# The last stores spread over the DMA engines, and the last tokens' rows as f32r passes in the slots' matmul stream

## The chip, the cores and the metric

The program runs on one NeuronCore of a Trainium2 chip. The core has TensorE (PE, with its weight loads shown apart as PEld), VectorE (DVE), ScalarE (ACT), GpSimd (POOL) and the sync engine (SP, whose queue issues all the transfers here), and 16 DMA engines that move the data. The metric is the device time of one execution in microseconds (us), the median of several runs.

## The reference

Three layers follow one another. In the first, 8 batches of 8 heads have 512 sequence tokens and 32 state slots of 64 values each; tokens read from the slots and slots from the tokens by softmax attention. The heads are joined to 512 channels, and each batch is then a sequence of 544 rows: 512 tokens, and behind them 32 slots. The second layer multiplies a linear projection by the sigmoid of a causal convolution over five rows and projects the product. The third does the work around which the change lies:

```python
h = np.maximum(x @ w_in, 0.0)                    # 512 -> 1024 channels
hp = pad(h, one zero row on either side)
conv_out = sum(conv_w[k] * hp[:, k:k + S, :] for k in range(3))
gate = 1.0 / (1.0 + np.exp(-conv_out))
return (h * gate @ w_out).astype(np.float32)     # 1024 -> 512, out is (8, 544, 512)
```

The convolution of the third layer looks one row ahead. So the last token of a batch (row 511) depends on its first slot (row 512), and cannot be finished with the other tokens.

## The kernel before

The channels lie on the partitions and the rows of the sequence on the free axis. Batch after batch, the tokens go through the attention and the second layer; `z_unit(b, f)` then computes one of eight groups f of 128 of the 1024 channels for the 512 tokens of batch b (a matmul block with tile names z<-g,wp, lines 161 to 163), its convolution and gate, and `o_unit(b, f)` adds that group to the four output banks of the batch (tiles o<-w,f, lines 452 to 454). Most large products are made of three f32r passes: both operands are split into a high and a low part, and high x high, high x low and low x high are added. In `outer` the two passes of a group's high part are lines 452 and 453, and the one with its low part is 454. ScalarE makes the high part and GpSimd subtracts it from the value for the low part (`low`, line 135).

After the eighth group of a batch, `store` scales the four banks into SBUF and the sync engine writes them out: three stores of 128 rows, and one of 127, because the last token is missing.

The slots of all batches are collected and worked on together at the end, as one block of 8 x 32 = 256 rows: `s_val`, `s_z` (tiles zs and t2s) and `s_o` (tiles os<-w,fs). `s_z(f)` has 33 rows per batch: the last token and the 32 slots. The last token's gated value is copied by GpSimd into a small tile el, 128 channels x 8 groups x 32 columns, of which 8 are used and the rest is zero (line 584). `s_last` multiplies it by `w_out` with plain f32 matmuls (L602), four groups of channels side by side at four column places of the array, into a third bank. `s_sum` copies that bank to SBUF, and `s_pick` adds the four places with one more f32 matmul against a matrix of zeros and ones called pick (L610), and stores the 8 rows.

The order of the work at the end is written out by hand in the string `CLOSING`: letters stand for units (v, z and o for the slots' `s_val`, `s_z`, `s_o`; Z and O for the tokens of the last batch; E, A, S, T for the last tokens' `s_ends`, `s_last`, `s_sum`, `s_pick`), and a bar ends half a step. A scheduler then fixes the order on each engine. The engines work through their queues in that order; a new z or zs block needs the only PSUM bank of its kind, which ScalarE must have read before (L443, L572).

Of the kernel before, what the change touches and what calls it, by code (L numbers as in the profile page):

```python
# [9 lines left out]
F32 = mybir.dt.float32  # L10
F32R = mybir.dt.float32r
# [3 lines left out]
AF = mybir.ActivationFunctionType  # L15
ALU = mybir.AluOpType
AX = mybir.AxisListType
PSUM = bass.MemoryType.PSUM

P = 128  # L20
# [18 lines left out]

CLOSING = """  # L40
v2 | E | v0 O v1 v3 Z Z O Z | O Z z2 z0 | O | | o0 | z1 O | | o1 Z z3 o2 z4 O Z | O Z | | O Z o4
z5 z6 z7 O | | o5 A0 o3 | | A1 S O o67 | T
"""


# [14 lines left out]
def tile_cross_attention_gated_conv_ffn(  # L60
# [19 lines left out]
    nc = tc.nc  # L80
    B, H, S, D = x.shape
    NS = state.shape[2]
    DM = H * D
# [5 lines left out]
    NFT = DF // P  # L89
# [7 lines left out]
    const = ctx.enter_context(tc.tile_pool(name="const", bufs=1))  # L97
    xp = ctx.enter_context(tc.tile_pool(name="xp", bufs=4))
    att = ctx.enter_context(tc.tile_pool(name="att", bufs=2))
# [4 lines left out]
    ps_z = ctx.enter_context(tc.tile_pool(name="ps_z", bufs=1, space=PSUM))  # L104
# [3 lines left out]
    ident = const.tile([P, P], F32, name="ident")  # L108
# [5 lines left out]
    for q in range(4):  # L114
        for g in range(NG):
            w = (q ^ g) % 2
# [4 lines left out]
    wv = const.tile([P, NCT, DM], F32, name="wv")  # L121
    wp = const.tile([P, 2, NCT, DF], F32R, name="wp")
    hl = const.tile([P, NFT, B, 2], F32, name="hl")
    pick = const.tile([P, B], F32, name="pick")
    nc.vector.reduce_sum(pick, ident.rearrange("p (j m) -> p m j", m=32)[:, 0:B, :], axis=AX.X)
    sT = const.tile([P, NCT, B, NS + HALO], F32, name="sT")

    s_tile = lambda name, shape=(P, S): att.tile(list(shape), F32, tag="s", name=name, bufs=7)
    t_tile = lambda name, shape=(P, S): cv.tile(list(shape), F32, tag="t", name=name, bufs=6)
# [4 lines left out]
    def low(out, v, hi, e=None):  # L134
        (e or nc.gpsimd).tensor_tensor(out=out, in0=v, in1=hi.bitcast(F32), op=ALU.subtract)  # L135
# [50 lines left out]
    A = {}  # L186
# [225 lines left out]
    O = {}  # L412
    W2 = {}

    def inner(ps, gs, f):
        c = slice(f * P, (f + 1) * P)
        for k in range(NCT):
            three(ps, wp[:, 0, k, c], wp[:, 1, k, c], gs[k][:, 0], gs[k][:, 1], k == 0, k == NCT - 1)

    def conv2(t, h, f, dve=False):  # L420

        if dve:
            nc.vector.tensor_scalar_mul(t, h(1), cw2(f, 1))
        else:
            nc.scalar.activation(t, h(1), AF.Copy, scale=cw2(f, 1))  # L425
        for k in (0, 2):
            nc.vector.scalar_tensor_tensor(  # L427
                out=t, in0=h(k), scalar=cw2(f, k), in1=t, op0=ALU.mult, op1=ALU.add
            )

    def gate2(ft, t, h):
        nc.scalar.activation(t, t, AF.Tanh, scale=0.5)  # L432
        nc.vector.scalar_tensor_tensor(out=t, in0=t, scalar=1.0, in1=h, op0=ALU.add, op1=ALU.mult)  # L433
        if ft is not None:
            nc.scalar.activation(ft[:, 0], t, AF.Copy)  # L435
            low(ft[:, 1], t, ft[:, 0])
# [14 lines left out]
    def outer(ps, ft, c, f):  # L451
        nc.tensor.matmul(ps, ft[:, 0, c], W2[f][:, 0], start=(f == 0), stop=False)  # L452
        nc.tensor.matmul(ps, ft[:, 0, c], W2[f][:, 1], start=False, stop=False)  # L453
        nc.tensor.matmul(ps, ft[:, 1, c], W2[f][:, 0], start=False, stop=(f == NFT - 1))  # L454

    def store(ps, n, dst, spare=False):

        if spare:
            ob = t_tile("ob")
            nc.vector.tensor_scalar_mul(ob[:n], ps[:n], 0.5)  # L460
        else:
            ob = cv.tile([P, DM], F32, tag="ob", name="ob", bufs=3)
            nc.scalar.activation(ob[:n], ps[:n], AF.Copy, scale=0.5)
        nc.sync.dma_start(out=dst, in_=ob[:n])

    def o_unit(b, f):
        if f == 0:
            O[b] = [ps_o.tile([P, DM], F32, tag="o", name="o") for _ in range(NT)]
        ft = F.pop((b, f))
        for t in range(NT):  # L470
            outer(O[b][t], ft, slice(t * P, (t + 1) * P), f)
        if f == NFT - 1:
            for t in range(NT):
                n = P if t < NT - 1 else P - 1
                store(O[b][t], n, out[b, t * P : t * P + n, :], b == B - 1 and t % 2)
            O.pop(b)
# [62 lines left out]
    FS = {}  # L539
    OS = []  # L540
    PARTS = [(0, 3), (3, 3), (6, 2)]

    EL = []

    def s_ends():

        EL.append(s_tile("el", (P, NFT, 32)))
        nc.gpsimd.memset(EL[0], 0.0)

    def s_val(ct):  # L550
        t = t_tile("t1s", (P, B, NS))
# [15 lines left out]
    def s_z(f):  # L567
        ps = ps_z.tile([P, B, NS], F32, tag="z", name="zs")
        inner(ps.rearrange("p b n -> p (b n)"), GS, f)
        h = s_tile("hs", (P, B, NS + 3))  # L570
        nc.gpsimd.memset(h[:, :, NS + 2 : NS + 3], 0.0)
        nc.scalar.activation(h[:, :, 2 : NS + 2], ps, AF.Relu, scale=0.5)  # L572
        if f == NFT - 1:
            yield 1
        nc.gpsimd.tensor_copy(h[:, :, 0:2], hl[:, f])
        t = s_tile("t2s", (P, B, N1))
        conv2(t, lambda k: h[:, :, k : k + N1], f)
        yield LATE
        gate2(None, t, h[:, :, 1 : 1 + N1])
        FS[f] = xp.tile([P, 2, N], F32R, tag="xn", name="fs")  # L580
        hi, lo = (FS[f][:, i].rearrange("p (b n) -> p b n", b=B) for i in range(2))
        nc.scalar.activation(hi, t[:, :, 1:], AF.Copy)
        low(lo, t[:, :, 1:], hi)
        nc.gpsimd.tensor_copy(EL[0][:, f, 0:B], t[:, :, 0])

    def s_o(*fs):
        if 0 in fs:
            OS.extend(ps_a.tile([P, DM], F32, tag="a", name="os") for _ in range(3))
        for i in range(2):
            for f in fs:  # L590
                outer(OS[i], FS[f], slice(i * P, (i + 1) * P), f)
            if NFT - 1 in fs:
                store(OS[i], P, out[B // 2 * i : B // 2 * (i + 1), S:, :], i)

    def s_last(h):

        fs = range(4 * h, 4 * h + 4)
        for j in range(2):
            for f in fs:
                q = 32 * (f - 4 * h)  # L600
                w = W2[f][:, j].bitcast(F32)
                nc.tensor.matmul(OS[2][q : q + 32], EL[0][:, f], w, start=h == j == 0, stop=h == j == 1)  # L602

    def s_sum():
        OS.append(t_tile("ol"))
        nc.scalar.activation(OS[3], OS[2], AF.Copy)

    def s_pick():
        ps = ps_z.tile([P, DM], F32, tag="z", name="ol")
        nc.tensor.matmul(ps[0:B], pick, OS[3], start=True, stop=True)  # L610
        store(ps, B, out[:, S - 1, :])


    live = []
# [27 lines left out]
    def half_steps(text):  # L642
        return [h.split() for h in text.split("|")]
# [25 lines left out]

    def closing():  # L670

        fns = {"v": s_val, "z": s_z, "o": s_o, "E": s_ends, "A": s_last, "S": s_sum, "T": s_pick}
        f = {"Z": 0, "O": -2}
        for h in half_steps(CLOSING):
            lots = [], []
            for t in h:
                late_lot = t in ("Z", "O") or bool(lots[1])
                if t in ("Z", "O"):
                    fn = z_unit if t == "Z" else o_unit
                    u = (fn, B - 1, f[t]) if f[t] >= 0 else (fn, B - 2, NFT + f[t])  # L680
                    f[t] += 1
                else:
                    u = (fns[t[0]], *map(int, t[1:]))
                lots[late_lot].append(u)
            yield lots

    def product1(c):
# [7 lines left out]
        out=craw[0 : K1 * NCT].bitcast(U64), in_=conv1_w.rearrange("k (c p) -> (k c) p", p=P)  # L695
    )
    nc.sync.dma_start(
        out=craw[32 : 32 + K2 * NFT].bitcast(U64), in_=conv2_w.rearrange("k (c p) -> (k c) p", p=P)
# [47 lines left out]
    for b in range(B):  # L746
        if b == B - 1:
            for units, end in closing():
                step(*units, end=end)
            break  # L750
        units = ahead(b)
        if b == 0:
            units = [u + v for u, v in zip(units, among())]
        for f in range(NFT):
            o = [(o_unit, b, f - 2)] if f >= 2 else [(o_unit, b - 1, NFT - 2 + f)] if b else []
            step(*units[2 * f], end=o)
            step(*units[2 * f + 1], end=[(z_unit, b, f)])
        A.pop(b)
# [30 lines left out]
```

## Time and profile before

| | |
|---|---|
| median of 3 runs | 611.78 us (611.67 to 613.34) |
| the profiled execution, its own time | 611.8 us |
| its span, first to last instruction | 610.0 us |
| TensorE busy | 558.1 us, 91% of the span, 3044 matmul records |
| VectorE, ScalarE, GpSimd busy | 447.8, 351.1, 297.7 us |
| DMA | 37.84 MB, mean 62 GB/s |

An instruction is busy from its start to its end in the profile. Matmuls overlap: one of 512 columns is shown with about 0.39 us, but the next one starts 0.23 us after it. For TensorE the distance of starts is therefore what a matmul takes of the time, and the shown duration is not. An f32 matmul is shown as two records. The time of the profiled execution is 1.8 us longer than its span; what lies outside the span has no instruction of the program.

### The profile page before, as it was taken

How to read it: one execution, taken by the hardware profiler on the slowest of the kernel's cores; microseconds unless marked ns; L12 is line 12 of the kernel's file. 1: busy time of each engine (PE TensorE's matmuls, PEld its weight loads, DVE VectorE, ACT ScalarE, POOL GpSimd, SP SyncE). 2: the span in 40 equal slices, each digit the busy share in tenths (PEclk: the TensorE clock that was granted, in tenths of full speed). 3: DMA queues.
4: the chain of work that ended last, by engine and by line, in shares of the span. 5: the costliest groups of instructions: out<-in, count | busy, mean ns of one | idle time of the engine just before them, and what ended most of it. 6: DMA issues, size and time to landing. Idle time of an engine off the chain costs nothing.

```text
span 610.0 us, 8741 instructions
## 1 busy us (share of the span) xinstructions
PE 558.1 (91%) x3044; PEld 408.4 (67%) x3044; DVE 447.8 (73%) x715; ACT 351.1 (58%) x665; POOL 297.7 (49%) x378
## 2 busy tenths in 40 slices
PE   1866798889999999999999999999999999999990
PEld 0632566566567777786778677767876788886760
DVE  5798699698688588757995798499849886453440
ACT  6687466656565566556655756475547655553540
POOL 4675679277462544254625454554436435342220
PEclk9986899989999999999999999999999999999996
DMA  6976002720116003601350144013001000100011
GB/s 227 349 232 108 5 5 79 151 48 10 53 41 114 9 2 93 117 3 59 61 94 9 58 75 78 10 59 80 2 1 65 6 2 0 70 0 1 1 57 48
DMA packets 97670, 37.84 MB, mean 62 GB/s; under 512 B 90158, under 2 KB 90202, under 8 KB 97626
## 3 DMA queue, kind: packets, MB, share of 16 engines
q1 hardware_dynamic: 97626, 37.29, 24.0%
q8 instruction: 24, 0.39, 0.3%
q14 instruction: 20, 0.16, 0.1%
HBM read 28.36 MB, written 8.91 MB: 61 GB/s over the span
## 4 chain that ended last, share of the span: by engine, by line
PE 76%; DVE 13%; ACT 3%; issue 2%; DMA 2%; POOL 0%; SPq 0%; DVEq 0%; POOLq 0%; ACTq 0%
PE o L452 10%; PE z L161 9%; PE o L454 9%; PE o L453 9%; PE z L162 9%; PE z L163 9%; DVE t L386 2%; PE val L161 2%; PE val L162 2%; PE val L163 2%; PE xr L371 2%; DVE t L427 2%; PE sw L237 2%; PE sc L237 1%; PE os L602 1%
## 5 line engine op out<-in xcount | busy, mean ns | idle before, releaser
L427 DVE SCALAR_TENSOR_TENSOR t<-h,cw,t 128x512 f32<-128x512 f32 x128 | 117.1, 918 | 54.8 <-ACT t L425 53.6
L452 PE MATMUL o<-w,f 128*128 128x512 f32 x256 | 104.0, 408 | 1.8 <-ACT f L435 1.6
L135 POOL TENSOR_TENSOR f<-t,f 128x512 fp32r<-128x512 f32 x64 | 89.8, 1404 | 31.4 <-ACT f L435 30.8
L161 PE MATMUL z<-g,wp 128*128 128x512 f32 x256 | 103.7, 405 | 0.0
L162 PE MATMUL z<-g,wp 128*128 128x512 f32 x256 | 101.6, 397 | 0.2 <-POOL g L135 0.2
L163 PE MATMUL z<-g,wp 128*128 128x512 f32 x256 | 101.6, 397 | 0.0
L453 PE MATMUL o<-w,f 128*128 128x512 f32 x256 | 99.9, 392 | 0.0
L386 DVE SCALAR_TENSOR_TENSOR t<-xr,cw,t 128x510 f32<-128x510 f32 (+3 forms) x128 | 90.2, 741 | 4.9 <-ACT sT L379 4.2
L432 ACT ACTIVATE t<-t 128x512 f32<-128x512 f32 x64 | 40.6, 634 | 78.7 <-DVE t L427 78.5
L454 PE MATMUL o<-w,f 128*128 128x512 f32 x256 | 77.8, 397 | 0.1
L135 POOL TENSOR_TENSOR g<-v,g 128x512 fp32r<-128x512 f32 (+1 forms) x36 | 46.5, 1292 | 41.0 <-ACT g L397 40.9
L433 DVE SCALAR_TENSOR_TENSOR t<-t,h 128x512 f32<-128x512 f32 x64 | 53.4, 835 | 15.8 <-ACT t L432 15.2
L452 PEld LDWEIGHTS o<-w,f 128*128 128x128 f32 x256 | 48.0, 188 | 25.2 <-ACT f L435 7.6
L435 ACT ACTIVATE f<-t 128x512 fp32r<-128x512 f32 x64 | 40.5, 633 | 41.0 <-DVE t L433 40.8
L161 PEld LDWEIGHTS z<-g,wp 128*128 128x128 f32 x256 | 48.3, 189 | 16.5 <-issue 2.1
L162 PEld LDWEIGHTS z<-g,wp 128*128 128x128 f32 x256 | 48.3, 189 | 12.6 <-POOL n L218 0.8
L163 PEld LDWEIGHTS z<-g,wp 128*128 128x128 f32 x256 | 48.3, 189 | 11.9 <-issue 0.4
L454 PEld LDWEIGHTS o<-w,f 128*128 128x128 f32 x256 | 46.8, 188 | 11.7 <-issue 1.6
L453 PEld LDWEIGHTS o<-w,f 128*128 128x128 f32 x256 | 48.2, 188 | 9.1
L442 POOL MEMSET h<- 128x2 f32 x64 | 6.4, 101 | 92.4 <-DVE t L433 91.4
L443 ACT ACTIVATE h<-z 128x512 f32<-128x512 f32 x64 | 38.2, 597 | 22.7 <-PE z L163 20.9
L425 ACT ACTIVATE t<-h,cw 128x512 f32<-128x512 f32 x63 | 45.9, 729 | 1.4
(165 smaller groups left out, 1017.4 us busy)
## 6 DMA issues: line engine op xcount, KB each, us to landing
xn<-in_x_dram SPq DMA_DIRECT2D x32, 256.0 KB, 4.4
out_dram<-ob SPq DMA_DIRECT2D x26, 256.0 KB, 2.2
y<-in_x_dram SPq DMA_DIRECT2D x96, 64.0 KB, 2.3
wir<-in_moe_w_in_dram SPq DMA_DIRECT2D x8, 512.0 KB
wor<-in_moe_w_out_dram SPq DMA_DIRECT2D x8, 512.0 KB, 10.2
wmr<-in_moe_w_out_dram SPq DMA_DIRECT2D x4, 512.0 KB, 3.2
wvr<-in_moe_w_val_dram SPq DMA_DIRECT2D x4, 512.0 KB, 6.9
out_dram<-ob SPq DMA_DIRECT2D x8, 254.0 KB
```

Source lines behind the costliest of these rows:

```text
L135: (e or nc.gpsimd).tensor_tensor(out=out, in0=v, in1=hi.bitcast(F32), op=ALU.subtract)
L161: nc.tensor.matmul(ps, wh, mh, start=first, stop=False)
L162: nc.tensor.matmul(ps, wh, ml, start=False, stop=False)
L163: nc.tensor.matmul(ps, wl, mh, start=False, stop=last)
L386: nc.vector.scalar_tensor_tensor(out=t[:, n:], in0=ps[r][:, 0 : S - n], scalar=cw1(ct, k), in1=t[:, n:], op0=ALU.mult, op1=ALU.add,)
L425: nc.scalar.activation(t, h(1), AF.Copy, scale=cw2(f, 1))
L427: nc.vector.scalar_tensor_tensor(out=t, in0=h(k), scalar=cw2(f, k), in1=t, op0=ALU.mult, op1=ALU.add)
L432: nc.scalar.activation(t, t, AF.Tanh, scale=0.5)
L433: nc.vector.scalar_tensor_tensor(out=t, in0=t, scalar=1.0, in1=h, op0=ALU.add, op1=ALU.mult)
L452: nc.tensor.matmul(ps, ft[:, 0, c], W2[f][:, 0], start=(f == 0), stop=False)
L453: nc.tensor.matmul(ps, ft[:, 0, c], W2[f][:, 1], start=False, stop=False)
L454: nc.tensor.matmul(ps, ft[:, 1, c], W2[f][:, 0], start=False, stop=(f == NFT - 1))
```

## The change

There are two edits. In `store`, a store of more than 16 rows whose destination has the rows as its outer dimension is issued in two parts: the largest multiple of 16 rows, and the rest (127 becomes 112 and 15). The two stores of the slots are written with the slot number outside and the batch inside, 32 x 4 rows instead of 4 x 32; for that the slots are put in that order when their high and low parts are made (tile fs), so these are now written with a stride of four.

The second edit removes `s_last`, `s_sum`, `s_pick` and the pick matrix. The last tokens' values are split into a high part (ScalarE) and a low part (GpSimd), 128 x 8 each, and `s_o` sends them through `outer` as its third bank, 8 rows, with the same three f32r passes as the slots: 24 small f32r matmuls (os<-w,el) in place of the 16 f32 ones and the pick.

```diff
-z5 z6 z7 O | | o5 A0 o3 | | A1 S O o67 | T
+z5 z6 z7 O | | o5 o3 | | O o67
...
-    pick = const.tile([P, B], F32, name="pick")
-    nc.vector.reduce_sum(pick, ident.rearrange("p (j m) -> p m j", m=32)[:, 0:B, :], axis=AX.X)
...
-        nc.sync.dma_start(out=dst, in_=ob[:n])
+        even = n // 16 * 16
+        if dst.shape[0] != n or n <= 16:
+            nc.sync.dma_start(out=dst, in_=ob[:n])
+        else:
+            nc.sync.dma_start(out=dst[:even], in_=ob[:even])
+            if n > even:
+                nc.sync.dma_start(out=dst[even:], in_=ob[even:n])
...
-        EL.append(s_tile("el", (P, NFT, 32)))
-        nc.gpsimd.memset(EL[0], 0.0)
+        EL.append(att.tile([P, NFT, 2, B], F32R, tag="s", name="el", bufs=7))
...
-        hi, lo = (FS[f][:, i].rearrange("p (b n) -> p b n", b=B) for i in range(2))
-        nc.scalar.activation(hi, t[:, :, 1:], AF.Copy)
-        low(lo, t[:, :, 1:], hi)
-        nc.gpsimd.tensor_copy(EL[0][:, f, 0:B], t[:, :, 0])
+        hi, lo = (FS[f][:, i].rearrange("p (h n b) -> p h b n", h=2, n=NS) for i in range(2))
+        tn = t[:, :, 1:].rearrange("p (h b) n -> p h b n", h=2)
+        nc.scalar.activation(hi, tn, AF.Copy)
+        low(lo, tn, hi)
+        hi, lo = EL[0][:, f, 0], EL[0][:, f, 1]
+        nc.scalar.activation(hi, t[:, :, 0], AF.Copy)
+        low(lo, t[:, :, 0], hi)
...
-        for i in range(2):
+        for i in range(3):
             for f in fs:
-                outer(OS[i], FS[f], slice(i * P, (i + 1) * P), f)
+                if i < 2:
+                    outer(OS[i], FS[f], slice(i * P, (i + 1) * P), f)
+                else:
+                    outer(OS[i][0:B], EL[0][:, f], slice(0, B), f)
             if NFT - 1 in fs:
-                store(OS[i], P, out[B // 2 * i : B // 2 * (i + 1), S:, :], i)
+                if i < 2:
+                    store(OS[i], P, out[B // 2 * i : B // 2 * (i + 1), S:, :].rearrange("b n d -> n b d"), i)
+                else:
+                    store(OS[i], B, out[:, S - 1, :])
...
-        fns = {"v": s_val, "z": s_z, "o": s_o, "E": s_ends, "A": s_last, "S": s_sum, "T": s_pick}
+        fns = {"v": s_val, "z": s_z, "o": s_o, "E": s_ends}
```

Three places show what that moves. The first is the end of TensorE's queue, before; w_1166, w_1244 and w_1318 are the parts of `w_out` of the groups 4, 6 and 7, fs are the slots, el the last tokens:

```order
L454 MATMUL os<-w_1244,fs 128x512 x2
L602 MATMUL os<-w_1318,el 32x512
L602 MATMUL os<-w_1166,el 32x512
L602 MATMUL os<-w_1241,el 32x512
L602 MATMUL os<-w_1244,el 32x512
L602 MATMUL os<-w_1318,el 32x512
L452 MATMUL os<-w_1318,fs 128x512
L453 MATMUL os<-w_1318,fs 128x512
L452 MATMUL os<-w_1318,fs 128x512
L453 MATMUL os<-w_1318,fs 128x512
L454 MATMUL os<-w_1318,fs 128x512 x2
L610 MATMUL ol<-ol,pick 8x512
```

and after, where w_1242 and w_1316 are the groups 6 and 7:

```order
L452 MATMUL os<-w_1242,fs 128x512 x2
L452 MATMUL os<-w_1242,el 8x512
L450 MATMUL os<-w_1316,fs 128x512
L451 MATMUL os<-w_1316,fs 128x512
L450 MATMUL os<-w_1316,fs 128x512
L451 MATMUL os<-w_1316,fs 128x512
L450 MATMUL os<-w_1316,el 8x512
L451 MATMUL os<-w_1316,el 8x512
L452 MATMUL os<-w_1316,fs 128x512 x2
L452 MATMUL os<-w_1316,el 8x512
```

The five f32 matmuls side by side and the pick have gone, and every slot block now has its el matmuls within it: two behind its high part and one behind its low part.

The second is the end of the sync engine's queue, before, with the last batch's stores, the two of the slots and that of the last tokens:

```order
L464 DMA out_dram<-ob 127x512
L464 DMA out_dram<-ob 128x512 x3
L464 DMA out_dram<-ob 127x512
L464 DMA out_dram<-ob 4x32x512 x2
L464 DMA out_dram<-ob 8x512
```

and after:

```order
L466 DMA out_dram<-ob 128x512 x3
L466 DMA out_dram<-ob 112x512
L468 DMA out_dram<-ob 15x512
L464 DMA out_dram<-ob 32x4x512 x2
L464 DMA out_dram<-ob 8x512
```

The 127 rows have become two issues, and the slots' stores have 32 as their outer dimension. The issues stand in the same order.

The third is the end of VectorE's queue, before; t2s<-hs,cw,t2s is the convolution of a slot block, t2s<-t2s,hs its gate, and ob<-o the copies of the last batch's output banks:

```order
L427 SCALAR_TENSOR_TENSOR t2s<-hs,cw,t2s 128x264 x2
L433 SCALAR_TENSOR_TENSOR t2s<-t2s,hs 128x264
L427 SCALAR_TENSOR_TENSOR t2s<-hs,cw,t2s 128x264 x2
L433 SCALAR_TENSOR_TENSOR t2s<-t2s,hs 128x264
L460 TENSOR_SCALAR ob<-o 128x512
L460 TENSOR_SCALAR ob<-o 127x512
L460 TENSOR_SCALAR ob<-os 128x512
```

and after:

```order
L425 SCALAR_TENSOR_TENSOR t2s<-hs,cw,t2s 128x264 x2
L458 TENSOR_SCALAR ob<-o 128x512
L458 TENSOR_SCALAR ob<-o 127x512
L431 SCALAR_TENSOR_TENSOR t2s<-t2s,hs 128x264
L425 SCALAR_TENSOR_TENSOR t2s<-hs,cw,t2s 128x264 x2
L431 SCALAR_TENSOR_TENSOR t2s<-t2s,hs 128x264
L458 TENSOR_SCALAR ob<-os 128x512
```

The two copies of the last batch's banks stood behind the last block's gate, and stand now ahead of the gate of the block before it.

## Rows read from the trace of the kernel before

**Rows 1.** Windows: us, busy us of each engine, clock, DMA share, GB/s.

```profile
530.00:596.30 66.30, 66.28 (x320) 47.38 (x318) 29.74 (x45) 29.74 (x60) 19.52 (x48) 1.00 0.04 16
596.30:610.00 13.70, 0.00 (x0) 0.00 (x0) 0.00 (x0) 0.59 (x1) 0.00 (x0) 0.58 0.18 51
```

**Rows 2.** The same view, a plain store and the last stretch of stores.

```profile
586.90:587.60 0.70, 0.70 (x5) 0.57 (x4) 0.67 (x2) 0.18 (x1) 0.06 (x1) 1.00 0.78 299
...
606.00:608.40 2.40, 0.00 (x0) 0.00 (x0) 0.00 (x0) 0.00 (x0) 0.00 (x0) 0.50 0.07 26
```

**Rows 3.** Waits of the sync engine's queue, 590 us on: us, times, longest.

```profile
SPq L784 <- DMA out_dram<-ob: 10.8, 1, 10.8
```

**Rows 4.** Line 464, store issues, 588:592 us and 596:600 us: ns min/median/max.

```profile
L464 SPq DMA_DIRECT2D out_dram<-ob x2: 254/294/333, 589.3 to 589.9; - x2
...
DMA to landing us min/median/max: 2.0/2.0/2.0
...
L464 SPq DMA_DIRECT2D out_dram<-ob x3: 539/672/830, 595.7 to 597.1; - x3
```

**Rows 5.** DMA issues of the whole span: count, KB each, us to landing.

```profile
out_dram<-ob SPq DMA_DIRECT2D x8, 254.0 KB
s<-in_state_dram SPq DMA_DIRECT2D x64, 8.0 KB, 1.7
```

**Rows 6.** Timeline of TensorE, one small group: start us, us, what.

```profile
564.27 0.40 PE L163 MATMUL z<-g,wp 128*128 128x512 f32 x1
564.60 1.05 PE L602 MATMUL os<-w,el 128*32 128x512 f32 x2
565.58 0.50 PE L452 MATMUL os<-w,fs 128*128 128x512 f32 x1
565.91 0.39 PE L453 MATMUL os<-w,fs 128*128 128x512 f32 x1
```

**Rows 7.** Timeline of TensorE, the group of five and the last block.

```profile
591.82 1.90 PE L602 MATMUL os<-w,el 128*32 128x512 f32 x10
593.66 0.50 PE L452 MATMUL os<-w,fs 128*128 128x512 f32 x1
594.00 0.39 PE L453 MATMUL os<-w,fs 128*128 128x512 f32 x1
...
594.69 0.63 PE L454 MATMUL os<-w,fs 128*128 128x512 f32 x2
```

**Rows 8.** Timeline of TensorE, f32r matmuls on half the rows (xr).

```profile
189.85 0.50 PE L371 MATMUL xr<-ah,nh 64*128 64x512 f32 x2
...
190.75 0.50 PE L452 MATMUL o<-w,f 128*128 128x512 f32 x1
191.08 0.39 PE L453 MATMUL o<-w,f 128*128 128x512 f32 x1
```

**Rows 9.** Groups by shape, span, then 520:597 us: busy us, mean ns.

```profile
L379 ACT ACTIVATE sT<-xr 128x4 f32<-128x4 f32 x32 | 5.6, 174 | 0.0
...
L135 POOL TENSOR_TENSOR fs<-t2s,fs 128x256 fp32r<-128x256 f32 x8 | 5.5, 689 | 2.2 <-ACT fs L582 2.1
...
L582 ACT ACTIVATE fs<-t2s 128x256 fp32r<-128x256 f32 x8 | 3.3, 416 | 2.3 <-DVE t2s L433 2.2
...
L584 POOL COPY el<-t2s 128x8 f32<-128x8 f32 x8 | 1.8, 225 | 14.1 <-DVE t2s L433 14.1
...
L606 ACT ACTIVATE ol<-os 128x512 f32<-128x512 f32 x1 | 0.6, 597 | 4.6 <-PE os L602 4.6
```

**Rows 10.** Timeline, the chain of the last slot block.

```profile
584.15 0.29 PE L163 MATMUL zs<-g,wp 128*128 128x256 f32 x1
...
588.73 0.42 ACT L582 ACTIVATE fs<-t2s 128x256 fp32r<-128x256 f32 x1 [0.50 <-DVE t2s L433]
```

**Rows 11.** Timeline, the last computation.

```profile
596.31 0.59 ACT L463 ACTIVATE ob<-ol 8x512 f32<-8x512 f32 x1 [0.60 <-PE ol L610]
```

More of the change, by code (lines that the diff above doesn't have):

```diff
@@ L588, in s_o @@
             OS.extend(ps_a.tile([P, DM], F32, tag="a", name="os") for _ in range(3))
-        for i in range(2):
+        for i in range(3):
             for f in fs:
-                outer(OS[i], FS[f], slice(i * P, (i + 1) * P), f)
+                if i < 2:
+                    outer(OS[i], FS[f], slice(i * P, (i + 1) * P), f)
+                else:
+                    outer(OS[i][0:B], EL[0][:, f], slice(0, B), f)
             if NFT - 1 in fs:
-                store(OS[i], P, out[B // 2 * i : B // 2 * (i + 1), S:, :], i)
[L595 to L611, printed above, removed]
+                if i < 2:
+                    store(OS[i], P, out[B // 2 * i : B // 2 * (i + 1), S:, :].rearrange("b n d -> n b d"), i)
+                else:
+                    store(OS[i], B, out[:, S - 1, :])
     live = []
```

## The prediction, on record before the run

> **What bounds the kernel now.** I read the windows by stage first, then the sync engine's waits, then the matmul rows of the last 50 us. In the closing stretch, 530 to 596.3 us, TensorE is busy 66.28 of 66.30 us at full granted clock; from 596.3 to 610.0 us, 13.7 us, no matmul runs, and one ScalarE copy is the only computation [rows 1]. So the kernel has two parts that decide here: a stretch set by TensorE, and a tail without computation. What ends the tail stands in the waits: the sync engine's last instruction waits 10.8 us for a store [rows 3]. Why the store takes that long shows in the DMA share. While a 128-row store runs, the 16 DMA engines are 78% busy at 299 GB/s; from 606 to 608.4 us the share is 0.07, about one engine of 16, at 26 GB/s [rows 2]. Eight stores have 127 rows, 254 KB [rows 5]; at 26 GB/s one takes 9.8 us. The last of them was issued at 589.9 us [rows 4], shortly before the two slot stores, so it is still running, on one engine, when these start, and what they put on that engine waits behind it. That is the reading on which the tail rests.
>
> **The tail.** The last of the three final stores is issued at 597.1 us [rows 4]; the span ends at 610.0, 12.9 us later. An ordinary 128-row store takes 2.0 us from issue to landing [rows 4]. After the landing the program still needs what it needs now: its wait of 10.8 us begins at 598.0, when the last issue ends (597.1 + 0.83), and ends at 608.8, so 1.2 us are left. With the 127-row stores cut into 112 and 15 rows and the slot stores written with 32 as the outer dimension, no engine has a long queue of its own. New tail behind the last issue: 2.0 + 1.2 = 3.2 us; gain 12.9 - 3.2 = 9.7 us.
>
> The bounds: an 8 KB load lands in 1.7 us [rows 5], so -0.3; the last issue itself took 0.83 us [rows 4] where an ordinary one is inside its 2.0, so up to +0.5. The last issue follows the end of the one before at once (0.67 + 0.54 us of issue from 595.7 on [rows 4], 16 rows' pattern now 32x4): if the new pattern is issued like a plain one in about 0.33 us, the estimate is 0.6 us less; if slower, more. I take today's 2.4 us from the first low-part matmul of the last block (594.69 [rows 7]) to the last issue, since the queue of issues sets it: ScalarE's copy of the 8 rows is done at 596.31 + 0.59 = 596.9 [rows 11], before 597.1. For that reason the removed pick matmul and its PSUM copy, though on the chain of waits, are worth nothing by themselves: their result already waits for the sync engine.
>
> The DMA page of the Trainium skill (DMA: Bandwidth & Descriptors, Why a DMA increments its semaphore by 16) says that a DMA uses the largest number of engines up to 16 that divides the outermost dimension on both sides. By it 127 rows get one engine and 4x32 four, as the low shares above agree; 112 and 32x4 would get 16 and 15 rows 15. No row here shows a 32x4 store, and the sum would be the same.
>
> **The matmuls of the last tokens.** Removed are 16 f32 matmuls (L602), in seven groups, five of one or two instructions and two of five. One group, start to start: the matmul ahead of it takes 0.33 us instead of 0.23, the group 0.98, the matmul behind it 0.33 [rows 6]; that is 0.98 + 0.10 + 0.10 = 1.18 us. A group of five takes 1.84 [rows 7], with the same edges 2.04. Sum: 5 x 1.18 + 2 x 2.04 = 9.98 us.
>
> Added are 24 f32r matmuls with 8 columns, 23 of them ahead of the last block's low part. Streaming 512 columns in f32r takes 0.23 us in the rows around (594.00 to 594.69, three in 0.69 us [rows 7]); f32r with half the array's rows also keeps 0.23 a round (xr: three rounds and one edge in 0.90 us [rows 8]). The edges are what the diff does not show. The old small matmuls had them too: in a group of five two rounds run one after the other (four column places), 1.84 - 0.98 = 0.86 us a round, so a group of one costs 0.98 - 0.86 = 0.12 within it and 0.20 at its neighbours, 0.32. For xr it is 0.90 - 0.69 = 0.21 plus 0.10 behind [rows 8] and, assumed, 0.10 ahead: 0.41. The order after has the new matmuls in 14 groups, 13 of them before the last low part. Taken at 0.32, the row nearest in width (32 columns): 23 x 0.23 + 13 x 0.32 = 5.29 + 4.16 = 9.45 us. Against 9.98 the matmuls give back only 0.5 us. Bounds: 10.62 at 0.41 (0.6 us slower than before), 5.29 with no edges (4.7 us gained).
>
> Here a page speaks against the change: the Trainium skill, TensorEngine Tiling (Array Packing), Key Properties, says that changing the tiling mode drains TensorE. The 0.33 us ahead of each small group agrees. By a reading with free passes the sum would be 4.2 us lower than mine.
>
> **Side work.** ScalarE gets eight copies of 128x8 and loses a 0.60 us copy; the nearest row is 128x4, 0.17 us, the upper end 0.42 of a 128x256 copy [rows 9]. GpSimd changes eight 128x8 copies (0.23) into subtractions, between that and 0.69 [rows 9]. The slot tiles are now written with a stride; contiguous they take 0.42 on ScalarE and 0.69 on GpSimd, and for the strided form I take the same, upper ends twice that. They hide behind TensorE's queue: in the closing stretch it never waits for them visibly. The tightest place is the last slot block. Today its high half is ready at 588.73 + 0.42 = 589.15, 5.0 us after the last projection matmul's start at 584.15 [rows 10]. In the new order 21 matmuls in six small groups stand between: 21 x 0.23 + 6 x 0.32 = 6.7 us. With the strided copy doubled and two small copies added it is 5.0 + 0.4 + 0.8 = 6.2, still covered; VectorE's two output copies, now ahead of the block before it, finish earlier than its matmuls need. Beyond that cover every us of delay is one us of the time. The smaller edits (a reduction at the start, a memset, seven extra issues in the long middle, where TensorE runs without waits for stores) I price at nothing: the reduction waits on an otherwise idle VectorE and the issues lie on a queue that waits for copies; uncovered, 0.2 and 0.3 us each once.
>
> **Sum.** 610.0 - 9.7 - 0.5 = 599.8 us of span. The profiled execution took 611.8, 1.8 more than its span, and the runs' median is 611.78, so nothing has to be corrected: 599.8 + 1.8 = 601.6 us. Own range, from -0.9 and +0.5 in the tail, +1.1 at the edges and 0.5 of stalls: 600.7 to 603.7.
>
> **Rivals.**
> A, no edges: the small matmuls slip between their neighbours for 0.23 each. 601.6 - 4.2 = 597.4 us. For it: the weights are a quarter as wide as those of L602. Against: every group of L602 and xr shows edges.
> B, the slot stores stay on four engines, so the change does not do all it says. Then 2 x 256 KB over four engines at 26 GB/s each [rows 2] is 5.0 us; the first is issued at 595.7 - 0.5 = 595.2, and with an estimated 1 us before its first row the data is out at 601.2, where my sum lands at 597.1 - 0.5 + 2.0 = 598.6: 2.6 us above mine, 604.2 us. For it: the store of today is low in share. Against: its outer dimension is what the diff turns.
> C, slower: f32r with 8 columns runs at the price of f32, 0.86 a round instead of 0.23. Then 23 x 0.63 = 14.5 us more, 616.1 us. Break-even with 611.8 lies at 10.2 / 23 = 0.44 more, 0.67 us a matmul. For it: no row has f32r with so few columns. Against: xr's rounds of 0.23.
> D, TensorE waits for the new copies at several slot blocks, about 2.5 us in all: 604 us.
>
> **Chances.** My forecast 0.73, A 0.12, B 0.06, D 0.05, C 0.03, anything else 0.01. A change under 0.3% (1.8 us) is what this kernel's measurement cannot tell from none. All but C and the remainder are faster by more: faster 0.95, same 0.02, slower 0.03. The range goes down to A and up to B: 597.0 to 604.5.
>
> **What would show it.** The DMA share in the last 3 us should be well above one engine and the sync engine's last wait about 2 us instead of 10.8. The last low-part matmul should start near 594.2. If the matmuls beside the 8-column groups are 0.23 apart, A holds; if an 8-column matmul is 0.8 long, C; if the share stays at four engines for 5 us, B; if GpSimd or ScalarE is named before os matmuls, D. I am wrong altogether if the wait behind the last issue stays above 5 us.

## The result, and the profile after

The changed kernel took 598.73 us (median of 4 runs, 597.21 to 599.61) beside 612.56 us of the kernel before (611.67 to 613.54): a ratio of 0.9771, 95% interval 0.9743 to 0.9799, 13.8 us less. The forecast was 601.6 us, with a range of 597.0 to 604.5. The time lies in the range, 2.9 us below the forecast. It lies 2.0 us below the narrower range that the forecast worked out for itself (600.7 to 603.7), and is inside the wide one only because that was stretched down to rival A.

The profiled execution took 597.21 us, its span 595.4, so 1.8 us lie outside the span as before. The windows of the changed kernel: the closing stretch of TensorE, the last two slot stores, and the whole tail (columns as in [rows 1]).

```profile
530.00:590.40 60.40, 60.37 (x306) 48.11 (x305) 29.31 (x44) 29.91 (x65) 20.78 (x45) 1.00 0.05 18
592.60:594.20 1.60, 0.00 (x0) 0.00 (x0) 0.00 (x0) 0.00 (x0) 0.00 (x0) 0.89 0.81 280
590.83:595.40 4.57, 0.00 (x1) 0.00 (x0) 0.50 (x1) 0.64 (x2) 0.00 (x0) 0.83 0.34 118
```

TensorE is as full as before and at full granted clock. Behind it come 4.6 us where [rows 1] had 13.7. The stores that moved 26 GB/s at the end [rows 2] now move 280, with 81% of the 16 DMA engines busy. The sync engine's last wait, the issues of the last three stores, and the landing, which answer to [rows 3, 4]:

```profile
SPq L779 <- DMA out_dram<-ob: 1.4, 1, 1.4
```

```profile
L464 SPq DMA_DIRECT2D out_dram<-ob x3: 448/546/668, 591.0 to 592.4; - x3
...
DMA to landing us min/median/max: 2.4/2.4/2.4
```

The wait of 10.8 us is 1.4 us. The last issue starts at 592.4, and the span ends 3.0 us later (before: 12.9). The stores of 254 KB [rows 5] are now 224 KB and land:

```profile
out_dram<-ob SPq DMA_DIRECT2D x8, 224.0 KB, 2.3
```

The small matmuls stand in the timeline of TensorE like any others. First the start of the slot matmuls in the kernel before, then the changed kernel's start and its last blocks (start us, shown us, what):

```profile
547.59 0.40 PE L452 MATMUL os<-w,fs 128*128 128x512 f32 x1
```

```profile
546.72 0.39 PE L450 MATMUL os<-w,fs 128*128 128x512 f32 x1
...
589.28 0.40 PE L451 MATMUL os<-w,fs 128*128 128x512 f32 x1
589.51 0.39 PE L450 MATMUL os<-w,el 128*8 128x512 f32 x1
589.74 0.39 PE L451 MATMUL os<-w,el 128*8 128x512 f32 x1
589.98 0.63 PE L452 MATMUL os<-w,fs 128*128 128x512 f32 x2
590.44 0.39 PE L452 MATMUL os<-w,el 128*8 128x512 f32 x1
```

All starts are 0.23 us apart. Ahead of a small group before it was 0.33, and as much behind it [rows 6]; here a group of el has no edge on either side.

With these rows the span of 610.0 us splits in three at the first slot matmul and at the first low part of the last slot block (594.69 before [rows 7], 589.98 after):

| stretch | before | after | difference |
|---|---|---|---|
| span's start to the first slot matmul | 547.59 | 546.72 | -0.9 |
| to the last block's low part | 47.10 | 43.26 | -3.8 |
| to the span's end | 15.3 | 5.4 | -9.9 |

The first line is not the change's. The changed kernel, profiled once more beside the experiments, began its slot matmuls at 548.20, 1.5 us later than here, and took the same 43.26 us (to 591.46) behind that. Between these two profiles, what varies lies ahead of the slots; the second line repeats to 0.01 us, and serves as the meter of the small matmuls below.

### The profile page after: what moved, and what is told of

Same layout as the page of the kernel before. It is cut to its first block, busy times and chain, and to the rows that moved or that the text cites. A ratio compares the mean times of both kernels' runs of the same rounds, so it can differ in the third digit from the quotient of the medians.

```text
span 595.4 us, 8734 instructions
## 1 busy us (share of the span) xinstructions
PE 553.4 (93%) x3034; PEld 410.8 (69%) x3034; DVE 447.9 (75%) x714; ACT 352.4 (59%) x672; POOL 299.8 (50%) x377
## 4 chain that ended last, share of the span: by engine, by line
PE 77%; DVE 10%; DMA 6%; SPq 3%; issue 2%; ACT 1%; POOL 0%; ACTq 0%; DVEq 0%
PE o L450 10%; PE z L159 10%; PE o L452 9%; PE o L451 9%; PE z L160 9%; PE z L161 9%; DMA wor<-in_moe_w_out_dram 3%; PE val L159 3%; PE val L160 2%; PE val L161 2%; PE xr L369 2%; DVE t L384 2%; PE sw L235 2%; DMA wvr<-in_moe_w_val_dram 2%; DMA wir<-in_moe_w_in_dram 2%
## 5 line engine op out<-in xcount | busy, mean ns | idle before, releaser
L425 DVE SCALAR_TENSOR_TENSOR t<-h,cw,t 128x512 f32<-128x512 f32 x128 | 118.7, 930 | 51.1 <-ACT t L423 49.9
L161 PEld LDWEIGHTS z<-g,wp 128*128 128x128 f32 x256 | 48.7, 190 | 11.8 <-issue 0.4
```

The source lines that it names most:

```text
L161: nc.tensor.matmul(ps, wl, mh, start=False, stop=last)
L425: nc.vector.scalar_tensor_tensor(out=t, in0=h(k), scalar=cw2(f, k), in1=t, op0=ALU.mult, op1=ALU.add)
```

## The experiments

**One edit of the stores at a time.** Three kernels ask whether both shapes make the tail. The first has the kernel before with this alone:

```diff
+        even = n // 16 * 16
...
+            nc.sync.dma_start(out=dst[:even], in_=ob[:even])
+            if n > even:
+                nc.sync.dma_start(out=dst[even:], in_=ob[even:n])
```

> The kernel before with the 127-row stores cut into 112 and 15 rows, and nothing else. Theory (both shapes make the tail: the 127-row store fills one engine's queue, and the slot stores use only four engines): what is left are two slot stores of 256 KB on four engines, 128 KB an engine at the 22 to 26 GB/s that one engine showed, 4.9 to 5.8 us from about 596.7 on, so the last store's wait ends near 602 and the time falls by 6 to 7 us, to about 606 (ratio 0.989). Rival 1 (only the four-engine slot stores matter, the 127-row store's engine is not in their way): no gain, 612.5. Rival 2 (only the 127-row store matters): the whole tail goes, 9.8 us, 602.8.

Measured: 609.71 us beside 612.81, ratio 0.9945 (0.9927 to 0.9962), about 3.4 us gained by the ratio (3.1 between the medians) where 6 to 7 were expected. The windows and the last wait:

```profile
597.00:599.00 2.00, 0.00 (x0) 0.00 (x0) 0.00 (x0) 0.00 (x0) 0.00 (x0) 1.00 0.24 27
599.00:602.00 3.00, 0.00 (x0) 0.00 (x0) 0.00 (x0) 0.00 (x0) 0.00 (x0) 0.85 0.37 98
602.00:605.00 3.00, 0.00 (x0) 0.00 (x0) 0.00 (x0) 0.00 (x0) 0.00 (x0) 0.50 0.17 62
```

```profile
SPq L790 <- DMA out_dram<-ob: 7.6, 1, 7.6
```

From 602 on a share of 0.17 moves 62 GB/s, 23 a busy engine, as assumed. But in the first two microseconds a share of 0.24, nearly four engines, moves only 27 GB/s: the engines count as busy and hardly move rows. That start was missing in the expectation. Both rivals fall, since neither nothing nor the whole tail was gained.

The second has the other edit alone:

```diff
-        hi, lo = (FS[f][:, i].rearrange("p (b n) -> p b n", b=B) for i in range(2))
+        hi, lo = (FS[f][:, i].rearrange("p (h n b) -> p h b n", h=2, n=NS) for i in range(2))
...
-                store(OS[i], P, out[B // 2 * i : B // 2 * (i + 1), S:, :], i)
+                store(OS[i], P, out[B // 2 * i : B // 2 * (i + 1), S:, :].rearrange("b n d -> n b d"), i)
```

> The kernel before with the slot stores written 32 x 4, and nothing else. Theory: the one engine with the 127 rows still has 254 KB from about 591 on, and behind them a sixteenth of each slot store, 32 KB: 286 KB at 22 GB/s are 13.0 us, the wait ends near 604.4 instead of 608.8, gain about 4.4 us, 608 us (ratio 0.993). Rival 1 (only the four-engine slot stores matter): gain 9.8 us, 602.8. Rival 2 (only the 127-row store matters): no gain.

Measured: 607.4 us, ratio 0.9908 (0.9879 to 0.9936), 5.6 us gained, somewhat more than the 4.4 expected. The last wait and the window before its end show one engine's 25 GB/s still at work:

```profile
SPq L785 <- DMA out_dram<-ob: 6.4, 1, 6.4
```

```profile
602.00:605.00 3.00, 0.00 (x0) 0.00 (x0) 0.00 (x0) 0.00 (x0) 0.00 (x0) 0.50 0.07 25
```

So the 127-row store alone keeps the program for 6.4 us, and the slot stores alone for 7.6; neither edit does without the other. The traces also hold the landings: a 127-row store reports its landing from one engine, a slot store of 4 x 32 from four, one of 32 x 4 from sixteen. In the kernel before, the 127-row store issued at 589.9 landed at 603.7, 13.8 us later. The third has both, with the f32 matmuls and the pick as before:

> The kernel before with both edits of the stores, and the plain f32 matmuls of the last tokens left as they were, with the pick. Theory: the whole tail goes and nothing else, 9.8 us, 602.8 us (ratio 0.984), with 3.0 to 3.2 us behind the last issue; the pick and its copy stay on the chain without a cost, because the last issue waits for the two ahead of it. Rival (the pick chain becomes the last wait, so that part of the tail's gain came from its removal): 0.5 to 1.5 us less gain, 604.

Measured: 602.79 us, ratio 0.9838 (0.9815 to 0.9862), 9.9 us gained, as expected. Its last wait:

```profile
SPq L791 <- DMA out_dram<-ob: 1.3, 1, 1.3
```

The span ends at 600.2, 5.4 us behind the last block's low part at 594.84; the changed kernel has 5.4 too. The pick, its copy and its matmul are still in this kernel and cost nothing: the rival falls. Measured in this way the first two kernels take 11.8 us (606.4 - 594.58) and 10.6 us (606.6 - 595.99) behind the low part, against 15.3 before: 3.5 and 4.7 us less, so that the second comes near the 4.4 expected.

**The matmuls alone.** The kernel after with the stores and the slot order of before:

```diff
-        hi, lo = (FS[f][:, i].rearrange("p (h n b) -> p h b n", h=2, n=NS) for i in range(2))
+        hi, lo = (FS[f][:, i].rearrange("p (b n) -> p b n", b=B) for i in range(2))
...
+        nc.sync.dma_start(out=dst, in_=ob[:n])
```

> The kernel after with the stores of the kernel before (127 rows in one, slot stores 4 x 32, slots in the old order). Theory: TensorE ends 4.7 us earlier than before, of which 3.8 is the small matmuls' gain; VectorE's last output copies, and with them the 127-row store, come some 7 us earlier, so that its one engine is through with them at about 594 to 595 and then has 128 KB of slot stores, until 599 to 601; the time is 601 to 604 us, a gain of 9 to 11 us, more than the 4 to 5 that the matmuls alone are worth, because the tail is shortened too. Rival (the tail is 12.9 us behind the last issue whatever comes before): gain 3.8 to 4.7 us, about 608.

Measured: 607.17 us, ratio 0.9908 (0.9889 to 0.9927), 5.6 us gained. My theory missed; the rival's 608 is nearer. The last 127-row store is issued at 584.1. Windows behind it, and the last wait:

```profile
586.00:588.00 2.00, 2.00 (x10) 1.35 (x9) 0.99 (x2) 0.90 (x2) 0.00 (x0) 1.00 0.05 7
588.00:592.00 4.00, 4.00 (x19) 2.60 (x18) 0.43 (x1) 0.57 (x3) 0.86 (x2) 1.00 0.07 26
...
597.00:602.00 5.00, 0.00 (x0) 0.00 (x0) 0.00 (x0) 0.00 (x0) 0.00 (x0) 0.50 0.27 74
```

```profile
SPq L772 <- DMA out_dram<-ob: 8.7, 1, 8.7
```

The single engine again starts slowly (7 GB/s for 2 us) before its 26 GB/s, so that from 586 to 592 it moves some 118 of 254 KB (2 x 7 + 4 x 26) and the slot stores meet it in spite of the earlier issue. Two numbers of this kernel matter below. Its last low part starts at 591.52, and its slot matmuls at 548.63: 42.89 us, against 47.10 before and 43.26 after. And the span ends 13.9 us behind the low part, 1.4 less than before.

**Type or width.** Why did the old small matmuls have edges and the new ones none? They differ in type (f32, f32r) and in columns (32, 8). One kernel widens el and stays with f32r:

```diff
-        EL.append(att.tile([P, NFT, 2, B], F32R, tag="s", name="el", bufs=7))
+        EL.append(att.tile([P, NFT, 2, 32], F32R, tag="s", name="el", bufs=7))
+        nc.gpsimd.memset(EL[0].bitcast(F32), 0.0)
...
-                    outer(OS[i][0:B], EL[0][:, f], slice(0, B), f)
+                    outer(OS[i][0:32], EL[0][:, f], slice(0, 32), f)
```

> The kernel after with the last tokens' tile el padded with zeros from 8 to 32 columns, still f32r: the same 24 matmuls, each with 128x32 weights as the old small f32 matmuls had. Theory W (width decides: 32 columns cost an edge of 0.33 us ahead of a group, whatever the type): the matmul ahead of each group is 0.33 from the next start, about 0.32 us a group, 13 groups, 4.2 us more than after, about 603. Theory T (the type decides: narrow f32 weights amid f32r have edges, narrow f32r has none): 0.23 at every neighbour, as in the kernel after, 598.7.

Measured, one run: 598.09 us. Its timeline of TensorE:

```profile
548.39 0.39 PE L451 MATMUL os<-w,fs 128*128 128x512 f32 x1
548.61 0.40 PE L450 MATMUL os<-w,el 128*32 128x512 f32 x1
548.85 0.40 PE L451 MATMUL os<-w,el 128*32 128x512 f32 x1
549.08 0.63 PE L452 MATMUL os<-w,fs 128*128 128x512 f32 x2
```

The other keeps 8 columns and goes back to f32:

```diff
+                    for j in range(2):
+                        nc.tensor.matmul(OS[i][0:8], EL[0][:, f], W2[f][:, j].bitcast(F32),
+                                         start=f == j == 0, stop=f == NFT - 1 and j == 1)
```

> The kernel after with the last tokens as plain f32 with 8 columns: 16 f32 matmuls (two a group of channels) in place of the 24 f32r ones, in seven places of the stream; the low part of el is not made. A round of f32 measured 0.86 us, so 16 x 0.86 = 13.8 us against 24 x 0.23 = 5.5, 8.3 us more. Theory T (type): edges of about 0.32 us at the seven groups come on top, 2.2 us, 609.2 us, and the matmul ahead of each group shows 0.33. Theory W (width): 8 columns have no edges, 0.23 ahead of each group, 607.0.

Measured, one run: 607.97 us, and in the timeline:

```profile
549.26 0.39 PE L450 MATMUL os<-w,fs 128*128 128x512 f32 x1
549.49 0.40 PE L451 MATMUL os<-w,fs 128*128 128x512 f32 x1
549.82 1.88 PE L600 MATMUL os<-w,el 128*8 128x512 f32 x4
551.63 0.72 PE L452 MATMUL os<-w,fs 128*128 128x512 f32 x2
...
600.77 0.40 PE L452 MATMUL os<-w,fs 128*128 128x512 f32 x1
601.10 1.88 PE L600 MATMUL os<-w,el 128*8 128x512 f32 x4
```

With 32 columns the f32r kernel has 0.23 or 0.24 ahead of each of its 14 groups; with 8 columns the f32 kernel has 0.32 or 0.33 ahead of each of its seven (549.49 to 549.82, 600.77 to 601.10), and a group of two f32 matmuls, four records, takes 1.81 (549.82 to 551.63), two rounds of 0.86 and 0.1 more. The theory of type holds, the theory of width falls. The f32 kernel's time lies between the two sums, and its single run does not decide; the matmuls do. From its first slot matmul to its last (548.80 to 600.77) are 51.97 us, against 43.49 in the kernel after (546.72 to 590.21): 8.5 more. With 14 f32 matmuls in six groups in that stretch, the prices of theory T give 14 x 0.86 + 6 x 0.32 - 23 x 0.23 = 8.7, and those of theory W 6.8. F32 by itself is not it either: a row of f32 matmuls with 128 columns (tile vals of the kernel before, 16 records) starts 0.24 us behind an f32r matmul. All the narrow f32r weights stood at the first columns of the array; other places were not tried.

```profile
505.45 0.40 PE L163 MATMUL z<-g,wp 128*128 128x512 f32 x1
505.69 3.62 PE L556 MATMUL vals<-sT,wv 128*128 128x256 f32 x16
```

**A store from another queue.** If the sync engine's issues set the end, one issue less should end sooner.

```diff
-            nc.sync.dma_start(out=dst, in_=ob[:n])
+            (nc.scalar if n <= 16 else nc.sync).dma_start(out=dst, in_=ob[:n])
```

> The kernel after with the last store (8 rows) issued from the queue of ScalarE, which made its rows, instead of the sync engine's. The sync engine's three last issues take 0.67 + 0.55 + 0.45 us one after the other; with two left, its last one starts at 591.79 instead of 592.43 and ScalarE's starts near 591.5. Theory (the queue of issues sets the end): 0.6 us less, 598.1 us. Rival (a first transfer on another queue lands later, or the landing of the second slot store sets the end anyway): within 0.2 us of the kernel after, or up to 1 us slower.

> The kernel after, unchanged, on the same chip as the three others, to compare them with: 598.7 us.

Measured on one chip: 598.63 us (ratio to before 0.9768, 0.9748 to 0.9788) and, for the unchanged kernel after, 599.83 (0.9789, 0.9770 to 0.9809). The intervals overlap, so the 1.2 us between the medians do not tell the two apart, and the traces have to. The issues and landings of the kernel with two queues:

```profile
L464 SPq DMA_DIRECT2D out_dram<-ob x2: 547/611/675, 592.9 to 593.7; - x2
L464 ACTq DMA_DIRECT2D out_dram<-ob x1: 705/705/705, 593.4 to 593.4; - x1
...
DMA to landing us min/median/max: 2.7/2.7/2.7
```

and of the kernel after beside it:

```profile
L464 SPq DMA_DIRECT2D out_dram<-ob x3: 457/547/670, 592.5 to 593.9; - x3
...
DMA to landing us min/median/max: 2.4/2.4/2.4
```

The sync engine's last issue does come earlier, 1.8 us behind the last low part (591.88 there) instead of 2.45. But a slot store lands in 2.7 us instead of 2.4, and the tail from the low part to the span's end is 5.6 us (597.5 - 591.9) as against 5.4. The shorter tail that the theory wanted is not there: what the earlier issue gave (0.6 us) was lost behind it, 0.3 us of it in that landing. Why a landing takes longer with two queues the rows do not say.

**Two passes instead of three.** If a narrow f32r matmul costs its 0.23 us and nothing else, fewer of them pay at once.

```diff
-        hi, lo = EL[0][:, f, 0], EL[0][:, f, 1]
+        hi, lo = EL[0][:, f, 0:B], EL[0][:, f, 32 : 32 + B]
...
+                    for j in range(2):
+                        nc.tensor.matmul(OS[i][0:40], EL[0][:, f], W2[f][:, j],
+                                         start=f == j == 0, stop=f == NFT - 1 and j == 1)
...
+                    nc.scalar.activation(ol[0:B], OS[i][32 : 32 + B], AF.Copy, scale=0.5)
+                    nc.vector.scalar_tensor_tensor(
+                        out=ob[0:B], in0=OS[i][0:B], scalar=0.5, in1=ol[0:B], op0=ALU.mult, op1=ALU.add
+                    )
```

> The kernel after with the high and low part of the last tokens side by side in one f32r weight tile of 40 columns (high in columns 0 to 7, low in 32 to 39, zeros between): two matmuls a group of channels in place of three, 16 instead of 24, the same weights for both; the rows of the low part come out at partitions 32 to 39 and are added behind the last matmul by a ScalarE copy and a VectorE addition. Ahead of the last block's low part stand 14 small matmuls instead of 23. Theory T (narrow f32r costs 0.23 and no edge, whatever its width): 9 x 0.23 = 2.1 us less from the first os matmul to the last low part, 41.2 instead of 43.25 us; the copy and the addition end about 2.4 us behind the last low part's start, just when the sync engine's third issue begins (2.45), so the tail stays 5.45 to 5.9 us; about 2 us less than the kernel after, ratio to before 0.975. Rival (40 columns are a wider tile and show edges of 0.32 us, 7 groups): 2.2 us given back, as the kernel after, 0.979.

Measured: 596.66 us (595.6 to 598.11) beside 613.0, ratio 0.9745 (0.9725 to 0.9765): faster than the kernel before, and below the ratios of the kernel after, 0.9771 and 0.9789, though the first one's interval overlaps it and these were taken in other sets of runs. The trace is sharper:

```profile
546.83 0.39 PE L450 MATMUL os<-w,fs 128*128 128x512 f32 x1
...
588.34 0.63 PE L452 MATMUL os<-w,fs 128*128 128x512 f32 x2
...
588.80 0.63 PE L603 MATMUL os<-w,el 128*40 128x512 f32 x2
...
589.39 1.31 SPq L464 DMA_DIRECT2D out_dram<-ob  x2
589.47 0.59 ACT L610 ACTIVATE ol<-os 8x512 f32<-8x512 f32 x1
590.09 0.68 DVE L611 SCALAR_TENSOR_TENSOR ob<-os,ol 8x512 f32<-8x512 f32 x1 [0.39 <-ACT ol L610]
590.79 0.45 SPq L614 DMA_DIRECT2D out_dram<-ob  x1
```

From the first slot matmul to the last low part it is 41.51 us instead of 43.26, 1.75 less; 2.1 were expected. The waits of TensorE show what is missing: one stall has grown.

```profile
PEld z L159 <- ACT h L441: 1.2, 1, 1.2
```

```profile
566.37 0.50 PE L159 MATMUL z<-g,wp 128*128 128x512 f32 x1 [0.75 <-ACT h L441]
```

Counted in the starts of TensorE's matmuls this wait costs 1.0 us here and 0.3 in the kernel after, which has one more of 0.3.

The tail is unchanged at 5.5 us (593.8 - 588.34): the new addition ends at 590.77, just as the sync engine comes free for the third issue.

## Why the prediction was right, and what failed in it

**The tail: right.** Forecast 9.7 us gained, measured 9.9; 3.2 us behind the last issue forecast, 3.0 measured, with 2.4 us between low part and last issue as before. Its reading, a one-engine store in front of slot stores on few engines, is shown by the first three experiments and the landings. The Trainium skill (DMA: Bandwidth & Descriptors, Why a DMA increments its semaphore by 16) had the engine counts; the near four engines' share for the old slot store and the 0.81 for the new one agree. What was too low is the price of few engines, which my second rival had at 2.6 us over the forecast: with the slot stores left on four engines the span ends 9.4 us behind the last issue (606.4 - 597.0), 6.4 more than with all. The slow start of such stores was missing. Had that rival come about, its time would have been some 3.6 us too low. The forecast's 9.8 us for a 127-row store were too few as well (13.8 measured), but no term of its sum rested on them.

**The small matmuls: the step that failed.** The forecast priced 13 groups of them at 0.32 us of edges, 4.16 us, from the row "nearest in width". Measured is no edge, 0.23 from start to start; rival A's mechanism is what happened, with 0.12 of the chance, by the sign that the forecast had named for it. So the forecast's time was right through the tail, and its range held the result by a bound borrowed from rival A; its own range had an upper bound for the edges, and none for their absence. Width was the wrong likeness. The two kernels on type and width show that f32r weights of 8 and of 32 columns have no edge and f32 weights of 8 have one; the two-pass kernel adds f32r with 40. The Trainium skill (TensorEngine Tiling (Array Packing), Key Properties) says that changing the tiling mode drains TensorE. For f32 groups the 0.33 agrees. For f32r the profile shows 128*8, 128*32 and 128*40 weights amid 128*128 ones, at 0.23: the measurement decides, and there is no drain to see. Whether such a matmul does not change the mode, or changes it without a price, no row tells. My other witness, xr, is f32r with edges [rows 8], but with 64 rows of weights in place of 128. It was no witness for narrow columns; whether its rows make its edge was not tried.

**Why 3.8 us and not rival A's 4.7.** The removed groups were worth 9.98 us; 23 matmuls at 0.23 are 5.29; 4.7 would be left, and 0.9 of it is missing. The weight loads' waits in the closing stretch of the changed kernel:

```profile
PEld z L159 <- ACT h L441: 0.5, 1, 0.5
PEld os L450 <- ACT el L589: 0.5, 1, 0.5
```

A weight load's wait is not yet time of the matmuls: in the kernel before, such waits of 0.8 us stand behind f32 groups and cost no more than the edges counted above. What these two cost shows in TensorE's starts. At the second wait they are

```profile
561.23 0.40 PE L161 MATMUL z<-g,wp 128*128 128x512 f32 x1
561.65 0.50 PE L450 MATMUL os<-w,fs 128*128 128x512 f32 x1
561.98 0.40 PE L451 MATMUL os<-w,fs 128*128 128x512 f32 x1
```

0.75 us for two matmuls, 0.29 more than two of 0.23; at the first wait (566.41, 566.80, 567.14) 0.27 more. On the other engines these grew (ns min/median/max), answering to [rows 9]:

```profile
L586 ACT ACTIVATE fs<-t2s x8: 652/657/675, 541.7 to 586.9; 128x256 fp32r<-128x256 f32 x8
L133 POOL TENSOR_TENSOR fs<-t2s,fs x8: 862/870/946, 542.4 to 587.7; 128x256 fp32r<-128x256 f32 x8
...
L589 ACT ACTIVATE el<-t2s x8: 200/204/217, 542.1 to 587.4; 128x8 fp32r<-128x8 f32 x8
L133 POOL TENSOR_TENSOR el<-t2s,el x8: 205/208/395, 543.3 to 588.5; 128x8 fp32r<-128x8 f32 x8
```

The strided slot tiles cost 0.66 us on ScalarE instead of 0.42 and 0.87 on GpSimd instead of 0.69, inside the bounds taken. They hide nearly everywhere, as forecast; one slot block waits for ScalarE. It is an earlier one, not the last, which the forecast called the tightest. There the forecast counted six small groups as cover, 6.7 us, where the order has four; the cover measured 5.0 us (583.61 to 588.59), and the high half was done at 587.6, a microsecond before it was needed. With the slot tiles contiguous again (the matmuls alone) the stretch is 42.89 instead of 43.26 us, so in this stream the stride costs about 0.4 us; beside the f32 matmuls it cost nothing (47.09 us, 547.75 to 594.84, in the kernel with both store edits, 47.10 before). It fits in the 0.5 us of stalls allowed in the forecast's own range, and is rival D at a sixth of its size. The other wait stays at about 0.3 us with contiguous tiles too; some 0.2 to 0.3 us are not located.

**Additivity.** The stores alone gained 9.9 us and the matmuls alone 5.6; together 13.8 to 14.0 by the ratio. With the old stores, the matmul edit also ran into the one-engine queue, so its 5.6 holds 4.2 us of matmuls and 1.4 of tail; with the stores mended it adds 602.79 - 598.73 = 4.1 between medians of different sets of runs, and 3.8 in the profiles (47.09 to 43.26 us, with 5.4 us of tail in both).

**The pick: right.** On the chain of waits, yet worth nothing: the kernel with both store edits keeps it and has the changed kernel's tail.

## What to carry to other kernels

A small group of matmuls should be priced by a row of its own type before one that is nearest in width (whether the rows of the weights count was not tried); where two rows differ in two properties, neither can be taken for a third case without saying which property is assumed to count. A store at the end of a program should be checked for the DMA share while it runs: a share of one or four engines at the end is worth microseconds, and mending one such store of two in a row gives only part. An instruction on the chain of waits is worth nothing by itself if the engine that it feeds is still busy when it ends, as the sync engine's queue was here.

## What the hardware showed that was not expected

- Narrow f32r weights (8, 32 and 40 columns of 128 rows) stand among 128-column ones at 0.23 us a matmul; f32 weights of 8 columns cost about 0.1 us at either neighbour, f32 weights of 128 columns nothing ahead of them (0.24).
- Stores on few engines start slowly: 27 GB/s in the first 2 us on nearly four engines before 23 an engine, 7 GB/s for 2 us on one before 26. The cause was not tried.
- Writes of 128x256 with a stride of four: ScalarE 0.66 us instead of 0.42; GpSimd, which also reads the high part with that stride, 0.87 instead of 0.69.
- A last store moved to a second queue brought the sync engine's last issue 0.6 us forward and left the tail no shorter (5.6 us beside 5.4).
